# Transposing attention probabilities by DMA, and fetching sampled value rows with GpSimd gathers, in a fused BigBird attention and GELU feed-forward kernel

## The chip, the cores and the metric

The kernel runs on one core of a Trainium2 chip. The metric is the device time of one execution in microseconds (us). The core has a matrix engine (TensorE, PE in the profile), a vector engine (VectorE, DVE), an activation engine (ScalarE, ACT), GpSimd (POOL), and SyncE (SP), which here only issues DMAs. Every engine works through its own instructions in order; semaphores connect them. SP, ACT and POOL issue DMAs into queues that share 16 DMA engines.

## The reference

Inputs are q, k, v of shape (4 batches, 8 heads, 768 positions, 64), three sampled key blocks for each of the 24 query blocks of 32 positions, and two weight matrices. Everything is float32 outside; the kernel works in bf16 with float32 accumulation.

```python
scores = q @ k.T / sqrt(64)                    # for each batch and head
mask[i, j] = (|blk_i - blk_j| <= 1) | (blk_i in (0, 23)) | (blk_j in (0, 23))
mask[block qb, block kb] = True                # for kb in sampled_blocks[qb]
attn = softmax(where(mask, scores, -1e9))
x = (attn @ v)                                 # heads joined: 3072 x 512
out = gelu_exact(x @ w_in) @ w_out             # 512 -> 2048 -> 512
```

So the first and the last query block attend to all 768 keys (dense), and every other block attends to three neighbouring blocks, the two end blocks and three sampled blocks, 256 keys in all (sparse).

## The kernel before

The work is cut into eight units: four batches, two halves (`hf`) of 384 query positions. The order is written out by hand. For each unit an attention stage is followed by FFN1 (`ffn1_step`, 8 steps of 8 products with `w_in` and a Gelu on ACT); FFN2 of that unit (`ffn2_pieces`, 24 pieces of 2 products) is cut up as filler for the attention stage of the next unit. `ffn2_last` computes the last one.

A unit's attention has eight groups (`unit_groups`): two dense groups (the dense block, half of the heads each), then five groups of two sparse blocks and one of a single block. For each group:

- `stage_scores` (L309): PE multiplies q with keys into a PSUM tile `sc` of pool psA (two buffers); for sparse blocks the keys are a window of `kT` (96 columns) and `kg` (160 columns: three sampled and two end blocks). DVE takes the maximum (`nm`, L329 or L336).
- `stage_exp` (L340): ACT writes the exponentials `pp` in bf16 (L347, four of 256 columns; L350 for dense).
- `stage_transpose` (L353): PE transposes `pp` in squares of 128x128 against an identity into PSUM (`tp`, L359; 8 squares for two blocks, 6 for a dense group, 4 for one block).
- `stage_evict` (L362): ACT, or DVE at every fourth turn, copies `tp` to SBUF as `ps` (L367, L369).
- `stage_av` (L372): PE multiplies `ps` with values; a column of ones in the values gives the denominator. DVE normalizes into `xh` (L394 to L401).
- `stage_x` (L407): PE transposes `xh`, DVE copies it into `xT` (L421), the input of FFN1.

`attention` (L469) runs these as a software pipeline. In step `it`, PE gets the scores of group it+1, AV of group it-1, a filler piece, the transposes of group `it`, `stage_x` of group it-2 and another filler piece; ACT gets the eviction of group `it` and the exponentials of group it+1.

Values for the sparse groups lie in SBUF tiles `vg0s` and `vg1s`, one of each for each half. Each batch's values are copied to a DRAM scratch `vscr` (L257) from which `v_window` fetches the neighbouring blocks (L282) and `v_sampled` the sampled ones (L265): one DMA of 32 rows, 33 KB, for each sampled block, its address from a register that SP or POOL loaded from a list of block numbers (`numbers_list`, `registers`, L205). A sampled block that is already covered is replaced by the block of zeros behind the values. `v_ends` copies the end blocks (L272 to L277). The order of value rows in `vg0s` and `vg1s` is that of the keys: window, then sampled, then ends. Tiles of a half are refilled for the next batch while the other half is worked on: `v_fetch` gives lists of steps, some run in FFN1 (`steps`), the rest in the attention stage (`later`). For unit 1 this is `second_values` (L556), called in step 5 of FFN1 of unit 0. In FFN1 before a new batch (`fresh`), `prep_pair` (L217) transposes that batch's q and k on PE; `k_sampled` (L247) copies sampled keys into `kg` on DVE and POOL.

Of the kernel before, what the change touches and what calls it, by code (L numbers as in the profile page):

```python
# [20 lines left out]
def kernel(  # L21
# [27 lines left out]

    nc = tc.nc  # L50
    P = 128
# [5 lines left out]
    assert NR == 3  # L57
    D_MODEL, D_FF = moe_w_in.shape
# [16 lines left out]
    ptpool = ctx.enter_context(tc.tile_pool(name="ptpool", bufs=3))  # L75
# [3 lines left out]
    psT = ctx.enter_context(tc.tile_pool(name="psT", bufs=2, space=PSUM))  # L79
    psO = ctx.enter_context(tc.tile_pool(name="psO", bufs=1, space=PSUM))  # L80
# [74 lines left out]
    first_v = load_v(0)  # L155
    first_v[2]()
    load_k(0, HALVES[1])
    load_q(0, HALVES[1], slice(0, 64))
    for f in first_v[:2]:
        f()  # L160
    for i in range(2):
        nc.vector.memset(vns[i][:, :, :, D:VW], 1.0)
        nc.vector.memset(vgl[i][64:P, :, D:VW], 1.0)
# [28 lines left out]

    def numbers_list(src, js, rs, engine):
# [4 lines left out]
        return idx.rearrange("o j r -> o (j r)"), js, rs, engine, NB if src is vf else NB - 1  # L198
# [18 lines left out]
    def prep_pair(b, which, pr, on_act, p0=0, p1=P, bank=None):  # L217

        src = nats[which, b]
        pool, tag = bank or (psT, "T")  # L220
# [40 lines left out]
    def v_sampled(b, j, r):  # L261
        queue, val = (nc.gpsimd, v_pool[j, r]) if (j, r) in v_pool else (nc.sync, v_sp[j, r])
        hf, u = (j - 1) // US, (j - 1) % US
        dst = vg0s[hf][96:128, u, :] if r == 0 else vg1s[hf][BL * r - BL:BL * r, u, :]
        queue.dma_start(out=dst, in_=vscr[b][bass.ds(val * BL, BL), :])  # L265
# [13 lines left out]
    def v_window(b, hf, a, z, queue=None):  # L279

        r0 = (US * hf + a) * BL
        (queue or nc.sync).dma_start(  # L282
            out=vg0s[hf][0:96, a:z, :],
            in_=bass.AP(tensor=vscr[b].tensor, offset=vscr[b].offset + r0 * VR,
                        ap=[[VR, 96], [BL * VR, z - a], [1, VR]]))

    def v_fetch(b, hf):

        j0 = 1 + US * hf

        def sampled(js):
            for j in js:
                for r in range(NR):
                    v_sampled(b, j, r)

        moved = [lambda a=a: v_window(b, hf, a, min(a + 3, US)) for a in range(0, US, 3)]
        return moved, [lambda a=a: sampled(range(a, min(a + 2, j0 + US)))
                       for a in range(j0, j0 + US, 2)]
# [10 lines left out]
    def stage_scores(b, hf, grp):  # L309
# [8 lines left out]
        if grp[0] == "sparse":  # L318
            js = grp[1:]
            A4 = A.rearrange("p (g j c) -> p j g c", j=2, g=2)  # L320
            for i, j in enumerate(js):
                for c0, c1 in ((0, 96), (96, 256)):
                    for hh in range(4):
                        rhs = (kT[:, hh, (j - 1) * BL:(j + 2) * BL] if c0 == 0
                               else kg[:, (j - 1) % US, hh, :])
# [14 lines left out]
    def stage_exp(grp):  # L340
# [8 lines left out]
        else:  # L349
            nc.scalar.activation(pp[:, 0:S], A[:, 0:S], AF.Exp, bias=nm[:, 0:1])  # L350
        st[grp] = pp

    def stage_transpose(grp):  # L353
        pp = st[grp]
        T = psT.tile([P, 8, P], BF16, name="tp", tag="T")
        n = 4 * (len(grp) - 1) if grp[0] == "sparse" else NT
        for c in range(n):
            cols = slice(c * P, (c + 1) * P) if grp[0] == "sparse" else slice(c, S, NT)
            nc.tensor.transpose(T[:, c, :], pp[:, cols], identity)  # L359
        st[grp] = (T, n)  # L360

    def stage_evict(grp, on_act):  # L362
        T, n = st[grp]
        ps = ptpool.tile([P, 8, P], BF16, name="ps")
        turn[0] += 1
        if on_act or turn[0] % 4:
            nc.scalar.copy(ps[:, 0:n, :], T[:, 0:n, :])  # L367
        else:
            nc.vector.tensor_copy(ps[:, 0:n, :], T[:, 0:n, :])  # L369
        st[grp] = ps  # L370
# [36 lines left out]
    def stage_x(hf, grp):  # L407
# [13 lines left out]
        nc.vector.tensor_copy(  # L421
# [26 lines left out]
    def ffn2_last(b, hf):  # L448

        banks = [(psA, "A"), (psT, "T"), (psA, "A"), (psT, "T"), (psO, "O"), (psV, "av")]  # L450
# [18 lines left out]
    def attention(b, hf, filler, extra, steps=(), head=5, started=False):  # L469
# [3 lines left out]
        for it in range(-1, n + 2):  # L473
# [184 lines left out]
```

## Time and profile before

| | |
|---|---|
| time, median of 3 runs | 350.5 us (350.29 to 351.52) |
| profiled execution: time, span | 350.54 us, 348.6 us |
| busy share of the span | PE 86%, ACT 63%, DVE 55%, POOL 39% |
| mean granted TensorE clock | 0.946 (1.00 from about 60 us on) |
| DMA moved | 42.27 MB, 121 GB/s on average |
| attention stage, steady units | 24.7 to 26 us |
| FFN1 stage | 10.4 us, 15 us where the next batch is prepared |
| FFN2 of the last unit, to the end | 13.6 us |

The page is of one execution. Busy time of PE is not time at its peak, because products overlap in it. In a group line the columns are: line, engine, operation, output tile and input tiles, shapes, count, then busy time and mean duration of one, then idle time just before them and what ended it.

### The profile page before, as it was taken

The page shows a single profiled execution, that of the slowest core. Times are in us where ns is not written, and L with a number is a line of the kernel's source. Part 1 is how long each engine was busy: PE and PEld are TensorE (multiplying, and loading weights), DVE is VectorE, ACT ScalarE, POOL GpSimd, SP SyncE. Part 2 cuts the span into 40 slices and gives each one's busy share as a digit, 9 for nine tenths or more (in the row PEclk, how much of TensorE's full clock was granted, in tenths as well). Part 3 has the DMA queues.
Part 4 walks back from the last instruction along what each step waited for, and adds up shares of the span by engine and source line. Part 5 has one row for each costly group of instructions (what it writes and reads, how often), then busy time and mean ns, then how long its engine had stood idle before and what let it go on. Part 6 is the DMA issues. An engine that isn't in the chain of part 4 may idle for free.

```text
span 348.6 us, 13273 instructions
## 1 busy us (share of the span) xinstructions
PE 300.2 (86%) x5284; PEld 168.5 (48%) x5284; DVE 191.6 (55%) x569; ACT 221.3 (63%) x370; POOL 134.4 (39%) x269
## 2 busy tenths in 40 slices
PE   6456789986998889977998989997998989998996
PEld 5233445443553445444454445444554545454575
DVE  7395543673774765266473766276473764276100
ACT  2364725785467776786557885697567876778540
POOL 7767609901488271777400410966101310000000
PEclk9655659999999999999999999999999999999999
DMA  7949999898388935898870313996440310000002
GB/s 102 148 148 193 198 198 166 162 235 190 125 192 141 211 91 187 183 174 142 161 167 0 73 49 125 200 184 145 109 104 2 81 40 32 0 35 34 30 22 72
DMA packets 43807, 42.27 MB, mean 121 GB/s; under 512 B 7969, under 2 KB 38690, under 8 KB 43746
## 3 DMA queue, kind: packets, MB, share of 16 engines
q0 software_dynamic: 22528, 17.55, 32.3%
q1 hardware_dynamic: 20786, 23.48, 24.5%
q8 instruction: 41, 0.67, 0.8%
q10 hardware_dynamic: 432, 0.39, 0.3%
q14 instruction: 20, 0.16, 0.1%
HBM read 45.63 MB, written 9.67 MB: 159 GB/s over the span
## 4 chain that ended last, share of the span: by engine, by line
PE 51%; ACT 20%; DMA 10%; issue 9%; DVE 4%; SPq 4%; POOL 1%; DVEq 0%; ACTq 0%; POOLq 0%
PE hp L429 21%; PE op L438 13%; ACT pp L347 10%; DMA vg<-vscr 6%; ACT ps L367 4%; PE tp L359 4%; PE av L388 4%; SPq L265 3%; PE op L459 3%; PE pt L224 3%; DMA vx<-in_v_dram 3%; PE sc L314 2%; ACT os L443 2%; ACT g L431 2%; ACT L431 1%
## 5 line engine op out<-in xcount | busy, mean ns | idle before, releaser
L438 PE MATMUL op<-w_out_sb,g 128*128 128x512 bf16 x336 | 95.0, 381 | 2.2 <-ACT os L443 1.6
L429 PE MATMUL hp<-xT,w_in_sb 128*128 128x384 bf16 x512 | 91.8, 332 | 0.9 <-ACT g L431 0.6
L265 POOL DMA_DIRECT2D vg<-vscr x108 | 57.5, 537 | 55.6 <-issue 23.0
L431 ACT ACTIVATE g<-hp 128x768 bf16<-128x768 f32 x64 | 51.7, 811 | 37.5 <-PE hp L429 37.4
L347 ACT ACTIVATE pp<-sc,nm 128x256 bf16<-128x256 f32 x176 | 69.0, 488 | 0.1
L329 DVE TENSOR_REDUCE nm<-sc 128x4 f32<-128x1024 f32 (+1 forms) x48 | 54.5, 1136 | 26.1 <-ACT ps L367 9.8
L367 ACT COPY ps<-tp 128x1024 bf16<-128x1024 bf16 (+1 forms) x48 | 45.2, 941 | 36.9 <-PE tp L359 36.9
L429 PEld LDWEIGHTS <-w_in_sb 128*128 128x128 bf16 x512 | 48.8, 99 | 36.4 <-issue 5.7
L251 POOL COPY kg<-kT 128x128 bf16 x106 | 25.9, 293 | 64.5 <-PE sc L314 56.1
L359 PE MATMUL tp<-identity,pp 128*128 128x128 bf16 x448 | 44.7, 230 | 6.7 <-ACT pp L350 3.2
L359 PEld LDWEIGHTS <-pp 128*128 128x128 bf16 x448 | 31.4, 107 | 29.0 <-ACT pp L347 9.0
L388 PE MATMUL av<-vg,ps 128*32 128x65 bf16 x1408 | 22.9, 200 | 20.2 <-ACT ps L367 9.2
L336 DVE TENSOR_REDUCE nm<-sc 128x1 f32<-128x768 f32 x16 | 15.3, 955 | 44.6 <-PE sc L314 44.6
L388 PEld LDWEIGHTS <-ps 128*32 128x32 bf16 x1792 | 19.5, 98 | 35.8 <-ACT ps L367 20.9
L438 PEld LDWEIGHTS <-g 128*128 128x128 bf16 x336 | 24.8, 98 | 20.9 <-issue 11.3
L314 PE MATMUL sc<-kT,qT 64*32 64x96 bf16 (+2 forms) x832 | 27.6, 236 | 3.5 <-ACT qT L236 2.8
L314 PEld LDWEIGHTS <-qT 64*32 64x32 bf16 x1536 | 14.1, 93 | 31.6 <-issue 26.1
L443 ACT COPY os<-op 128x512 f32<-128x512 f32 x21 | 12.4, 593 | 25.8 <-PE op L438 25.8
L401 DVE TENSOR_TENSOR xh<-av,rec 128x256 bf16<-128x256 f32 (+1 forms) x64 | 22.9, 358 | 2.2
L234 DVE COPY kT<-pt 128x768 bf16<-128x768 bf16 x14 | 13.4, 956 | 16.5 <-PE pt L224 16.4
L394 DVE TENSOR_SCALAR den<-av 128x4 f32<-128x4 f32 (+1 forms) x64 | 9.9, 155 | 20.1 <-PE av L388 20.1
L314 PE MATMUL sc<-kg,qT 64*32 64x160 bf16 x704 | 18.2, 240 | 2.0 <-issue 1.8
(67 smaller groups left out, 277.5 us busy)
## 6 DMA issues: line engine op xcount, KB each, us to landing
vg<-vscr SPq DMA_DIRECT2D x20, 297.0 KB, 5.2
out_dram<-os SPq DMA_DIRECT2D x21, 256.0 KB, 2.1
vg<-vscr SPq DMA_DIRECT2D x156, 33.0 KB, 4.4
vg<-vscr POOLq DMA_DIRECT2D x108, 33.0 KB, 4.1
kn<-in_k_dram POOLq DMA_DIRECT2D x8, 384.0 KB, 6.4
vx<-in_v_dram POOLq DMA_DIRECT2D x8, 384.0 KB, 9.5
vscr<-vn SPq DMA_DIRECT2D x3, 792.0 KB, 3.3
qn<-in_q_dram POOLq DMA_DIRECT2D x6, 384.0 KB, 7.8
```

What stands on the lines that cost most here:

```text
L251: copy(kg[:, (j - 1) % US, :, BL * r:BL + BL * r], kTs[b % 2][:, :, bass.ds(vals[j, r] * BL, BL)])
L265: queue.dma_start(out=dst, in_=vscr[b][bass.ds(val * BL, BL), :])
L314: nc.tensor.matmul(out_, lhsT=qT[rows, h // 2, j * BL:(j + 1) * BL], rhs=rhs[rows], start=True, stop=True)
L329: nc.vector.tensor_reduce(out=nm[:, 0:2 * n].rearrange("p (j g) -> p j g", g=2), in_=A4[:, 0:n], op=ALU.max, axis=AX.X, negate=True)
L347: nc.scalar.activation(pp[:, 256 * n:256 * n + 256], A[:, c:c + 256], AF.Exp, bias=nm[:, n:n + 1])
L359: nc.tensor.transpose(T[:, c, :], pp[:, cols], identity)
L367: nc.scalar.copy(ps[:, 0:n, :], T[:, 0:n, :])
L388: nc.tensor.matmul(av[32 * hh:32 * hh + 32, s, :], lhsT=probs[:, 32 * hh:32 * hh + 32], rhs=vals[:, VW * h:VW * h + D + 1], start=(c == 0) ...
L401: nc.vector.tensor_tensor(xh[:, at:at + n, :], av[:, 0:n, 0:D], rec[:, 0:n, None].to_broadcast([P, n, D]), op=ALU.mult)
L429: nc.tensor.matmul(hp[:, i, 0:UT], lhsT=w_in_sb[:, ki, (m + i) * P:(m + i + 1) * P], rhs=xT[:, ki, :], start=(ki == 0), stop=(ki == KIN - 1))
L431: nc.scalar.activation(g[:, m:m + 2, :], hp[:, :, 0:UT], AF.Gelu)
L438: nc.tensor.matmul(op, lhsT=g[:, m, t * P:(t + 1) * P], rhs=w_out_sb[:, m, :], start=(m == 0), stop=(m == KOUT - 1))
```

## The change

- Probabilities: `stage_transpose` issues one transposing DMA on SP, from `pp` in SBUF to `ps` in SBUF (8, 6 or 4 squares at once). The PE transposes, the PSUM tile `tp` and `stage_evict` are gone. The dense exponentials are written in the order that the DMA needs.
- Pipeline: in step `it` the transposing DMA of group it+1 follows its exponentials, AV is of group it-2 and `stage_x` of group it-3; there is one step more. Two filler pieces come after AV in every step (four in the first). The copy to `xT` moves from DVE to ACT. ACT loads the Gelu table after the last exponentials of a unit.
- PSUM: psT has one buffer and psO two; `prep_pair` rotates over them.
- Sampled values: one indirect gather of POOL for each block, 96 rows, with row numbers computed on the chip (`value_rows`) in place of three DMAs with register addresses. Sampled rows now come first in the order (96 rows of `vg0s`), then the window (split over `vg0s` and `vg1s`, two DMAs), then the ends. Sparse scores are computed in three column slices (96, 96, 64) in place of two (96, 160).
- Order: values of unit 1 are fetched at the start of FFN1 of unit 0; loads of q and k move from the attention stage to FFN1; values of batch 0 are loaded with their end blocks last; some copies move between POOL and DVE.

```diff
-    ptpool = ctx.enter_context(tc.tile_pool(name="ptpool", bufs=3))
+    ptpool = ctx.enter_context(tc.tile_pool(name="ptpool", bufs=4))
...
-    psT = ctx.enter_context(tc.tile_pool(name="psT", bufs=2, space=PSUM))
-    psO = ctx.enter_context(tc.tile_pool(name="psO", bufs=1, space=PSUM))
+    psT = ctx.enter_context(tc.tile_pool(name="psT", bufs=1, space=PSUM))
+    psO = ctx.enter_context(tc.tile_pool(name="psO", bufs=2, space=PSUM))
...
-    first_v = load_v(0)
-    first_v[2]()
     load_k(0, HALVES[1])
     load_q(0, HALVES[1], slice(0, 64))
-    for f in first_v[:2]:
+    for f in load_v(0):
         f()
...
+    def value_rows():
+        vfb = const.tile([1, NB, NR], BF16, name="vfb")
+        nc.vector.tensor_copy(vfb, vf)
+        ones = const.tile([1, SW], BF16, name="ones")
+        nc.vector.memset(ones, 1.0)
+        seen = psV.tile([SW, NB, NR], F32, name="seen", tag="av")
+        nc.tensor.matmul(seen.rearrange("p j r -> p (j r)"), lhsT=ones,
+                         rhs=vfb.rearrange("p j r -> p (j r)"), start=True, stop=True)
+        for r in range(NR):
+            rows = slice(BL * r, BL * r + BL)
+            nc.vector.tensor_scalar(vrows[rows], seen[rows, :, r], float(BL), pcol[rows, 0:1],
+                                    op0=ALU.mult, op1=ALU.add)
...
-    def v_sampled(b, j, r):
-        queue, val = (nc.gpsimd, v_pool[j, r]) if (j, r) in v_pool else (nc.sync, v_sp[j, r])
+    def v_sampled(b, j):
         hf, u = (j - 1) // US, (j - 1) % US
-        dst = vg0s[hf][96:128, u, :] if r == 0 else vg1s[hf][BL * r - BL:BL * r, u, :]
-        queue.dma_start(out=dst, in_=vscr[b][bass.ds(val * BL, BL), :])
+        nc.gpsimd.indirect_dma_start(
+            out=vg0s[hf][0:SW, u, :], out_offset=None, in_=vscr[b][:, :],
+            in_offset=bass.IndirectOffsetOnAxis(ap=vrows[:, j:j + 1], axis=0))
...
-                for c0, c1 in ((0, 96), (96, 256)):
+                for c0, c1 in ((0, SW), (SW, 192), (192, 256)):
...
     def stage_transpose(grp):
         pp = st[grp]
-        T = psT.tile([P, 8, P], BF16, name="tp", tag="T")
+        ps = ptpool.tile([P, 8, P], BF16, name="ps")
         n = 4 * (len(grp) - 1) if grp[0] == "sparse" else NT
-        for c in range(n):
-            cols = slice(c * P, (c + 1) * P) if grp[0] == "sparse" else slice(c, S, NT)
-            nc.tensor.transpose(T[:, c, :], pp[:, cols], identity)
-        st[grp] = (T, n)
...
+        nc.sync.dma_start_transpose(out=ps[:, 0:n, :], in_=pp[:, 0:n * P])
         st[grp] = ps
...
-        nc.vector.tensor_copy(
+        nc.scalar.copy(
             xT[:, :, t0:t0 + n * BL].rearrange("p h (j q) -> p j h q", j=n),
...
-        for it in range(-1, n + 2):
+        for it in range(-1, n + 3):
             if it + 1 < n and not (started and it == -1):
                 stage_scores(b, hf, groups[it + 1])
-            if 0 <= it - 1 < n:
-                stage_av(b, hf, groups[it - 1])
-            for _ in range(head if it == -1 else int(it <= n)):
+            if 0 <= it - 3 < n:
+                stage_x(hf, groups[it - 3])
+            if 0 <= it - 2 < n:
+                stage_av(b, hf, groups[it - 2])
+            for _ in range(4 if it == -1 else 2):
                 next(filler, None)
-            if 0 <= it < n:
-                stage_transpose(groups[it])
-                stage_evict(groups[it], started and it < 3)
             if it + 1 < n:
                 stage_exp(groups[it + 1])
-            if 0 <= it - 2 < n:
-                stage_x(hf, groups[it - 2])
-            if it >= 0:
-                next(filler, None)
+                stage_transpose(groups[it + 1])
+            elif it + 1 == n:
+                nc.scalar.activation(warm, identity[:, 0:1], AF.Gelu)
...
     def second_values():
-        v_sp.update(block_numbers(vf, J1, (0, 1), SP))
-        for a in range(0, US, 4):
-            v_window(0, 1, a, min(a + 4, US))
-            for j in J1[a:a + 4]:
-                for r in range(NR):
-                    v_sampled(0, j, r)
+        moved, rows = v_fetch(0, 1)
+        for f in moved + rows:
+            f()
         for f in load_qk(1) + load_v(1):
             f()
...
             if u == 0:
                 k_dve |= block_numbers(ids, J1, (2,), DVE)
-                k_pool = block_numbers(ids, J1, (0, 1), POOL)
-                v_pool |= block_numbers(vf, J1, (2,), POOL)
+                k_pool |= block_numbers(ids, J1, (0, 1), POOL)
+                second_values()
...
-                if u == 0 and s == 5:
-                    k_dve |= block_numbers(ids, J0[5:], RS, DVE)
-                    second_values()
                 if s == 4 and nxt and not fresh:
                     v_ends(b, 1, nc.vector.tensor_copy)
+                if s == 6 and u > 0 and nxt and not fresh and b + 1 < B:
+                    v_ends(b + 1, 0, nc.vector.tensor_copy)
```

## Prediction

> **What bounds the kernel now.** I read the head of the page and its groups first, then one steady round in the timeline, then the DMA issues in a quiet and in a busy stretch, then the chain where it leaves its regular pattern. The groups that matter (instruction, tiles, shapes, count | busy us in all, mean ns | idle before, releaser):
>
> ```profile
> PE 300.2 (86%) x5284; PEld 168.5 (48%) x5284; DVE 191.6 (55%) x569; ACT 221.3 (63%) x370; POOL 134.4 (39%) x269
> ...
> L438 PE MATMUL op<-w_out_sb,g 128*128 128x512 bf16 x336 | 95.0, 381 | 2.2 <-ACT os L443 1.6
> ...
> L347 ACT ACTIVATE pp<-sc,nm 128x256 bf16<-128x256 f32 x176 | 69.0, 488 | 0.1
> ...
> L367 ACT COPY ps<-tp 128x1024 bf16<-128x1024 bf16 (+1 forms) x48 | 45.2, 941 | 36.9 <-PE tp L359 36.9
> ...
> L359 PE MATMUL tp<-identity,pp 128*128 128x128 bf16 x448 | 44.7, 230 | 6.7 <-ACT pp L350 3.2
> ```
>
> PE is busy 86% of the span. L347 and L367 show what ACT does in attention: exponentials, and three of four evictions of the transposed probabilities; their idle columns and that of L359 show ACT waiting for PE's transposes and PE for ACT's exponentials. A unit (one batch, half of the queries) is an attention stage of eleven loop steps, with FFN2 of the unit before as filler, and an FFN1 stage. From the first score product to the first FFN1 product the attention stages of units 0 to 7 last 29.7, 29.1, 26.9, 27.9, 25.9, 25.7, 25.9 and 24.7 us. Busy time of each engine in four steady rounds of unit 6, each from one group's first score product to the next group's:
>
> ```profile
> core 0: us, PE busy (x) PEld busy (x) DVE busy (x) ACT busy (x) POOL busy (x), PEclk, DMA share, GB/s
> 271.07:273.38 2.31, 2.23 (x69) 1.24 (x68) 1.63 (x4) 1.93 (x6) 1.00 (x4) 1.00 0.57 164
> 273.38:276.30 2.92, 2.52 (x78) 1.41 (x77) 2.25 (x6) 2.92 (x8) 1.00 (x4) 1.00 0.24 47
> 276.30:278.62 2.32, 2.30 (x79) 1.41 (x78) 2.16 (x6) 1.08 (x3) 1.00 (x4) 1.00 0.44 80
> 278.62:281.77 3.15, 2.73 (x79) 1.46 (x78) 2.64 (x7) 3.15 (x7) 1.00 (x4) 1.00 0.14 24
> ```
>
> Mean 10.70/4 = 2.68 us. In the two long rounds ACT is busy from end to end, as in
>
> ```profile
> 278.24 1.01 ACT L367 COPY ps<-tp 128x1024 bf16<-128x1024 bf16 x1 [1.24 <-PE tp L359]
> ...
> 279.15 1.57 ACT L347 ACTIVATE pp<-sc,nm 128x256 bf16<-128x256 f32 x4
> ```
>
> The eviction and the four exponentials are 2.6 of a round. The clock is 1.00 throughout.
>
> **Part by part, a steady round.** PE loses eight transposes. In the chain eight in a run take 0.46 us (121.02); 44.7 us over 56 such eights is 0.80, the rest being the wait for the last exponential. It gains 16 score products, since the slices are three now, not two: batches of eight start 0.06 to 0.07 us apart (271.07, 271.13, 271.20), so 0.15. What is left on PE: scores 0.5, AV 0.36, two filler pieces of 0.48 (ten FFN2 products in a run take 2.26), transposes of the output 0.1: 1.9 us. ACT loses an eviction of 1.01 in three rounds of four, and gains the copy to xT, which DVE does in 0.29; by the exponentials of the same width, four in 1.58, it is 0.4 on ACT. With the output's copy of 0.59 three times in ten rounds, ACT comes to 1.58 + 0.4 + 0.2 = 2.2. DVE, without its quarter of the evictions (0.69) and the xT copy, keeps the maximum 1.23, then 0.15 + 0.18 + 0.42 with gaps: 2.1. The engines are level, so I take 2.25 us a round, 0.43 less than now, over six rounds -2.6 us a unit.
>
> The price is the new path: exponentials, SP's issue, the transfer, AV. The trace has no transposing DMA. The nearest row is a store of as many bytes, 256 KB from SP, issue to landing, in unit 7's quiet stage (the DMA issues of 300 to 327 us; the last column is the landing):
>
> ```profile
> q1 hardware_dynamic: 432, 0.79, 7.7%
> ...
> out_dram<-os SPq DMA_DIRECT2D x3, 256.0 KB, 2.0
> ```
>
> and from 134 to 171 us, where loads for the next batch run:
>
> ```profile
> out_dram<-os SPq DMA_DIRECT2D x2, 256.0 KB, 6.3
> ```
>
> So 2.0 at the lower end. At the other end are pieces: a row of the source gives eight pieces of 256 bytes, 1024 in all. From the q1 line (packets, MB, share of 16 rings), 0.077 x 27 us x 16 / 432 = 77 ns a packet of 1.8 KB; over the whole span SP's and ACT's queue shows 0.245 x 348.6 x 16 / 20786 = 66 ns at about 1.1 KB. The straight line through both gives some 52 ns for 256 bytes, 64 pieces an engine: 3.3 us, and with issue and landing 5. I take 3.3 us from issue to landing, nearer the store, which is the same bytes from the same queue.
>
> Where that lands: AV of a group stands two rounds behind its exponentials in PE's order (loop index it+1 against it-2), so PE reaches it one round and the next scores later: 2.25 + 0.6 = 2.9 us after the exponentials end, if PE is on time. The loop from one end of exponentials through transfer, AV 0.36, fillers 0.95, scores 0.5, maximum 1.23, exponentials 1.58 and semaphores 0.3 spans four rounds: (3.3 + 4.9)/4 = 2.05, below 2.25. It decides only above 4.1 us. But at the end of a unit nothing is left to hide the last group's transfer: PE has two thin steps (AV 0.36, filler 0.95, output transposes 0.1: 1.4 each, 2.8) before that group's AV, which comes 3.3 and semaphores 0.3 after the exponentials. I charge 0.8. So -1.8 us a unit where DMA is quiet (units 2, 4, 6, 7): -7.2. In units 1, 3 and 5 the SP queue also carries value windows and POOL's gathers share the rings; I take half, -2.7. Behind a transpose that waits for its exponentials on SP stand the output stores and the windows; the stores are read by nobody, the windows only a unit later.
>
> The Trainium skill puts a transposing DMA at 261 GB/s where measured (DMA: Bandwidth & Descriptors, Latency and other measured facts), which would be 1.0 us of data for 256 KB, an estimate from that page; with the 2.0 of the store it would make 3.0 from issue to landing, 0.3 less at the end of seven units, so 336. No run here shows it yet.
>
> **Sampled values.** 264 transfers of 33 KB become 88 gathers of 96 rows, all from POOL. A gather costs POOL between 0.54 (one of today's issues) and 1.6 us (three of them); I take 0.9, as one 384 KB load costs 0.8 (537 ns is the mean of L265's 108 on POOL). From unit 2 on they run a unit ahead: no cost. Moved without cost too: the broadcast of the end blocks from POOL (4.58) to DVE (1.52), beside an FFN1 stage in which DVE is busy 2.0 of 9.0 us (134 to 143), and 54 key copies from DVE (0.20) to POOL (0.29), which has 40 us a unit; if POOL were late with them, PE would wait in the sparse scores. Unit 0: now the value copy in DRAM lands at 23.2 and POOL's first fetch goes at 23.9. After the change, POOL first waits for the two end blocks, now loaded behind the values (16.1), then does 0.62 + 4.58 + 4.38 us of copies, so gathers run from 26 to 37.6 with two weight loads between (33.6 or 45.3 at the ends), landing 4 us later; today's last AV is at 44.9. With a pipeline one round longer: +2, between 0 and +6. Unit 1 is where the chain leaves its pattern:
>
> ```profile
> 65.92 6.07 DMA vg<-vscr
> 72.01 5.78 DMA vg<-vscr
> 78.10 2.63 issue
> ```
>
> The fetches of unit 1 are issued from 62 us on, after register loads, and PE waits; its stage is 4.1 us longer than 25. The change issues them ahead of FFN1 of unit 0. But the loads for batch 1 then follow at once in POOL's queue, and the one for q must wait until the second half of q has been transposed at 60.9; POOL's 22 kg copies (5.25) stand behind it, and unit 1's sparse scores wait for those. I count -2. Unit 3 has one such wait of 1.9 at 159.6: -1. Loading the Gelu table ahead saves the 0.15 us PE stall in each FFN1: -1.
>
> **Sum.** The profiled execution was 350.54 (span 348.6 and 1.94 around it), the median 350.5: -7.2 - 2.7 + 2 - 2 - 1 - 1 = -11.9, so 338.5 us.
>
> **Rivals.**
> *Late transposes (slower).* The 6.3 us store shows what the SP queue does beside loads. If issue to landing is 5.5, the loop gives (5.5 + 4.9)/4 = 2.6 a round, +0.35 over six, and the end of the unit waits 2.2 more: 4.3 a unit over the forecast, seven units: 338.5 + 30 = 368. It decides from about 4.6 us on, where round and end together eat the 1.8. For it: median 4.4 us for the small fetches of today. Against: quiet stores at 2.0 in four units. 0.17.
> *Pieces bound the queue (slower).* At 3.3 us of ring time each, transposes go no faster than that: two dense ones of 2.5, five of 3.3, one of 1.7 make 23.2, with 3.4 ahead and 4 behind 30.6, 5.7 more than 24.9: about 350 + 8 x 5.7 = 396. 0.10.
> *Squares one by one.* If each 128x128 square were a transfer of its own after the last, at 1.3 us (the 1.9 us that a 33 KB fetch takes in quiet, less the landing that overlaps), 56 squares take 73 us a unit: about 350 + 8 x 50 = 750. 0.03. The Trainium skill's row for the DMA path, 1309 ns for one square against 390 on TensorE (VectorE: DVE Perf Modes, The three transpose paths), speaks for it; the trace's 2.0 us for eight times the bytes speaks against.
> *Gain given back on POOL.* Gathers of 1.6 us put unit 0 at +6, and unit 1 keeps its wait: 338.5 + 4 + 5 = 348 or a little more. 0.12, split evenly between a small gain, no change and a small loss.
>
> **How the numbers follow.** Forecast 0.58, its own range 322 to 347: the lower end if transposes land within 2.5 us and the rounds come down to the PE's 1.9. A measurement tells 0.5% (1.75 us) from no change. Faster: 0.57 of the forecast and 0.04 of the last rival, 0.61. Same: 0.01 and 0.04, 0.05. Slower: 0.17 + 0.10 + 0.03 + 0.04, 0.34. The range runs from just below the forecast's own to the queue-bound case, 320 to 398; the squares, half of the queue-bound case and a tail below are left out.
>
> **What would show it.** Right: no L359 or L367 left; steady rounds of 2.2 to 2.4 us; transposes landing in 3 to 4 us after issue; PE waiting for ps only at a unit's end; unit 1's stage under 28. Wrong: AV waiting for the transposes in every round, SP's issue rows lasting over 2 us, or the first FFN1 product of unit 0 after 50 us.

## The result, and the profile after

The changed kernel takes 488.9 us (median of four runs, 481.8 to 493.1) where the kernel before takes 351.0 beside it: a ratio of 1.383, with a 95% interval of 1.359 to 1.407. The ratio counts only runs within 1.5% of the fastest of their kernel (481.8 and 488.7 us here; 356.3 us is left out before), and so do all ratios below. The forecast was 338.5 us, and the range ended at 398. The profiled execution took 493.05 us with a span of 491.0, the longest of the four; two later profiles of the same kernel (486.4 and 484.1 us) show the same rows.

The page of the changed kernel, engines first, then groups (line, engine, operation, tiles, count | busy us in all, mean ns | idle before, releaser):

```profile
PE 295.1 (60%) x5485; PEld 160.4 (33%) x5541; DVE 177.0 (36%) x447; ACT 241.2 (49%) x386; POOL 158.6 (32%) x300
...
L285 POOL DMA_INDIRECT vg<-vscr,vrows x88 | 83.0, 943 | 158.8 <-issue 73.4
...
L446 PE MATMUL op<-w_out_sb,g 128*128 128x512 bf16 x280 | 88.9, 442 | 12.8 <-issue 12.8
...
L368 ACT ACTIVATE pp<-sc,nm 128x768 bf16<-128x768 f32 x16 | 58.2, 3709 | 35.2 <-DVE nm L354 33.6
...
L396 PE MATMUL av<-vg,ps 128*32 128x65 bf16 x1408 | 22.2, 208 | 52.9 <-DMA ps<-pp 52.1
L354 DVE TENSOR_REDUCE nm<-sc 128x1 f32<-128x768 f32 x16 | 15.3, 955 | 96.3 <-remote 62.7
```

TensorE still has some 300 us of work, now in 491. Its mean granted clock is 0.80 where it was 0.95, and an FFN2 product (L446) lasts 442 ns in place of 381, so a part of each loss below can be the lower clock. L359 and L367 are gone. Three things took their place. The dense exponentials (L368) last 3.71 us each; before the change they lasted 0.90 (count, shortest, median and longest in ns, first and last start, shapes):

```profile
L350 ACT ACTIVATE pp<-sc,nm x16: 882/904/907, 19.7 to 304.3; 128x768 bf16<-128x768 f32 x16
```

AV (L396) stands idle 52 us for the transposing DMA. And the dense maxima (L354) wait 63 us for "remote", which no instruction or transfer in the trace explains. The waits for the DMA are few and long. These are the two longest pieces of that kind in the chain that ended last (start, duration):

```profile
48.17 29.13 DMA ps<-pp x2
...
302.63 11.98 DMA ps<-pp
```

The attention stages of units 0 to 7, from the first score product to the first FFN1 product, last 65.0, 35.6, 44.8, 37.2, 46.6, 38.0, 37.4 and 32.2 us; before the change none was over 31. FFN1 of unit 1, with gathers beside it, lasts 27.4 us in place of 14.5. (Read in the same way, unit 0 took 30.7 us before, not the 29.7 of the prediction.)

### The profile page after: what moved, and what is told of

Read it like the earlier page. It is cut to its first block, busy times and chain, and to the rows that moved or that the text cites. A ratio compares the mean times of both kernels' runs of the same rounds, so it can differ in the third digit from the quotient of the medians.

```text
span 491.0 us, 13019 instructions
## 1 busy us (share of the span) xinstructions
PE 295.1 (60%) x5485; PEld 160.4 (33%) x5541; DVE 177.0 (36%) x447; ACT 241.2 (49%) x386; POOL 158.6 (32%) x300
## 4 chain that ended last, share of the span: by engine, by line
PE 33%; DMA 22%; another core or an unknown queue 17%; DVE 10%; ACT 10%; issue 6%; DVEq 1%; POOL 0%; POOLq 0%; SPq 0%; ACTq 0%
DMA ps<-pp 21%; PE hp L437 15%; PE op L446 7%; ACT pp L368 5%; PE av L396 3%; ACT pp L365 3%; DVE nm L354 3%; PE sc L331 2%; PE op L467 2%; DVE kg L273 2%; PE pt L246 2%; DVE nm L347 2%; PE tx L426 1%; ACT os L451 1%
## 5 line engine op out<-in xcount | busy, mean ns | idle before, releaser
L285 POOL DMA_INDIRECT vg<-vscr,vrows x88 | 83.0, 943 | 158.8 <-issue 73.4
L446 PE MATMUL op<-w_out_sb,g 128*128 128x512 bf16 x280 | 88.9, 442 | 12.8 <-issue 12.8
L368 ACT ACTIVATE pp<-sc,nm 128x768 bf16<-128x768 f32 x16 | 58.2, 3709 | 35.2 <-DVE nm L354 33.6
L331 PE MATMUL sc<-kg,qT 64*32 64x96 bf16 (+1 forms) x1408 | 31.6, 228 | 69.5 <-ACT pp L368 43.6
L273 POOL COPY kg<-kT 128x128 bf16 x160 | 39.7, 299 | 76.8 <-DVE kT L256 43.4
L331 PEld LDWEIGHTS <-qT 64*32 64x32 bf16 x2240 | 25.6, 100 | 112.1 <-issue 62.3
L396 PE MATMUL av<-vg,ps 128*32 128x65 bf16 x1408 | 22.2, 208 | 52.9 <-DMA ps<-pp 52.1
L354 DVE TENSOR_REDUCE nm<-sc 128x1 f32<-128x768 f32 x16 | 15.3, 955 | 96.3 <-remote 62.7
L396 PEld LDWEIGHTS <-ps 128*32 128x32 bf16 x1792 | 21.2, 107 | 72.6 <-DMA ps<-pp 65.6
L446 PEld LDWEIGHTS <-g 128*128 128x128 bf16 x336 | 29.5, 107 | 39.0 <-issue 19.3
L429 ACT COPY xT<-tx 128x256 bf16<-128x256 bf16 (+1 forms) x56 | 19.7, 352 | 45.9 <-PE tx L426 45.7
L331 PE MATMUL sc<-kT,qT 64*32 64x96 bf16 (+2 forms) x832 | 33.6, 253 | 6.8 <-ACT qT L258 3.0
L426 PE MATMUL tx<-identity,xh 128*128 128x128 bf16 x96 | 16.2, 240 | 10.1 <-DVE xh L409 6.9
L258 ACT ACTIVATE qT<-pt 128x768 bf16<-128x768 bf16 (+1 forms) x16 | 11.6, 730 | 18.8 <-PE pt L246 14.4
```

Source lines behind the costliest of these rows:

```text
L273: copy(kg[:, (j - 1) % US, :, BL * r:BL + BL * r], kTs[b % 2][:, :, bass.ds(vals[j, r] * BL, BL)])
L285: nc.gpsimd.indirect_dma_start(out=vg0s[hf][0:SW, u, :], out_offset=None, in_=vscr[b][:, :], in_offset=bass.IndirectOffsetOnAxis(ap=vrows[ ...
L331: nc.tensor.matmul(out_, lhsT=qT[rows, h // 2, j * BL:(j + 1) * BL], rhs=rhs[rows], start=True, stop=True)
L354: nc.vector.tensor_reduce(out=nm[:, 0:1], in_=A[:, 0:S], op=ALU.max, axis=AX.X, negate=True)
L368: nc.scalar.activation(pp[:, 0:S].rearrange("q (t p) -> q p t", t=NT), A[:, 0:S].rearrange("q (p t) -> q p t", t=NT), AF.Exp, bias=nm[:, 0:1])
L396: nc.tensor.matmul(av[32 * hh:32 * hh + 32, s, :], lhsT=probs[:, 32 * hh:32 * hh + 32], rhs=vals[:, VW * h:VW * h + D + 1], start=(c == 0) ...
```

## The experiments

Eighteen runs were made on five chips, A to E; those on one chip were made one after another. The kernel before took 350.7 to 352.6 us on each of them, so ratios can be compared between chips. One thing cannot, as will be seen. Stage lengths are read as above. "Pauses" are idle times of TensorE of over 0.3 us, beside a gather, ahead of an instruction that waits for nothing; how near to a gather still counts moves a sum by some us.

### One part undone at a time (chip A)

**Dense exponentials in rows.**

```
-  pp[:, 0:S].rearrange("q (t p) -> q p t", t=NT), A[:, 0:S].rearrange("q (p t) -> q p t", t=NT)
+  pp[:, 0:S].rearrange("q (t p) -> q t p", t=NT), A[:, 0:S].rearrange("q (p t) -> q t p", t=NT)
```

> The changed kernel with one edit: the dense exponentials write 128 consecutive elements at a time and read every sixth element of PSUM, in place of the reverse. Theory: the 16 exponentials of 3.71 us (0.90 before) lie on the path at the head of each unit; they fall to 0.9 to 1.2 us and the time falls by 16 x 2.6 = 42 us, to 440 to 455. Rival, that the head of a unit waits for the late reduces and transposes anyway: the exponentials fall as far, the time by under 15 us. Rival, that ACT is as slow over a strided read as over a strided write: they stay over 3 us and the time at 482 to 493.

430.5 us, ratio 1.220 (1.209 to 1.231), some 10 us under the theory's range; the chip turned out to have a part in that. The group of this kernel:

```profile
L368 ACT ACTIVATE pp<-sc,nm 128x768 bf16<-128x768 f32 x16 | 14.4, 898 | 14.7 <-DVE nm L354 14.3
```

The same elements, written side by side and read with a stride from PSUM, cost 0.90 us. The strided bf16 write was the whole of the 2.8 us by which one exponential had grown.

**Plain transfers for the gathers.**

```
-  nc.gpsimd.indirect_dma_start(out=vg0s[hf][0:SW, u, :], ..., in_offset=IndirectOffsetOnAxis(ap=vrows[:, j:j + 1], axis=0))
+  nc.gpsimd.dma_start(out=vg0s[hf][0:SW, u, :], in_=vscr[b][(j - 1) * BL:(j + 2) * BL, :])
```

> The changed kernel with each gather replaced by a plain transfer of 96 neighbouring rows on the same queue; it leaves the choice of rows out, with the same bytes into the same places. Theory: the indirect form holds up DVE and PE (62.7 us of waits of the dense reduces that no engine's work explains, 15.9 and 17.3 in two other rows); they go and the time falls by 50 to 90 us, to 400 to 440. Rival, that the load of 100 KB per gather on the rings is what delays everything: the waits stay and the time is 475 to 495. Rival in between, that only POOL's 0.94 us per gather is gained: 2 to 8 us in units 0 and 1, 480 to 487.

443.6 us, ratio 1.263 (1.255 to 1.270), just above the theory's range, and no remote wait is left. I took this for the theory. Most of the 45 us was the chip: the changed kernel never ran on this one, and the repeats below show what that means.

**Squares on TensorE again, straight after their exponentials.** `stage_transpose` as before the change with the eviction behind it, dense exponentials in plain order, psT with two buffers and psO with one.

> The changed kernel with the squares transposed on TensorE and evicted by ACT and DVE again, with the PSUM banks as before the change and the dense exponentials in plain order; the gathers and the schedule stay. Theory of three losses: the waits for the transposing DMA (60.9 us) and the slow exponentials (45 us) go, the stalls beside the gathers stay (60 to 90 us), PE and ACT have more to do: 385 to 430. Rival, that the transposing DMA is the cause of all three: 340 to 365 with no unexplained waits of the reduces. Rival, that the gathers are: over 440.

432.7 us, ratio 1.233 (1.226 to 1.240). It says little: TensorE reached each group's transposes while ACT was still at its exponentials, and every stage, also that of unit 7 with nothing beside it (34.6 us), was long. The kernel further down with the transposes one round later is the proper undo.

**Both of the first two.**

> The dense exponentials written in rows and the gathers replaced by plain transfers of 96 neighbouring rows (the choice of rows left out), the transposing DMA kept. Theory: the two losses add up, 488 - 42 - 50 to 90 = 356 to 396, and what is left over 350 is the transposes delayed behind other transfers. Rival, that they overlap (the slow exponentials hide behind the stalls): within 10 us of the better of the two kernels that have one edit each.

424.3 us, ratio 1.207 (1.200 to 1.214). Beside each other on one chip, the exponentials are worth 19.3 us here (443.6 to 424.3) and the indirect form 4.5 (ratio 1.220 to 1.207). What is left, 73 us over the kernel before, is neither. Two windows of this kernel's DMA issues, unit 0 and then unit 7 (queues: packets, MB, share of 16 engines; issues: count, median us to landing):

```profile
q0 software_dynamic: 5264, 5.70, 55.8%
q1 hardware_dynamic: 9968, 4.88, 51.7%
...
ps<-pp SPq DMA_TRANSPOSE x8, 14.6
```

```profile
q1 hardware_dynamic: 7734, 2.41, 55.1%
...
ps<-pp SPq DMA_TRANSPOSE x8, 4.0
```

Beside the weights on POOL's queue a transpose takes 14.6 us from issue to landing, alone 4.0. Stages: 63.6 us for unit 0, 25.1 for unit 7.

### Again, and the traffic (chip B)

**The changed kernel again.**

> The changed kernel itself once more, for a second trace. The two edits so far were worth 58 and 45 us alone and 65 together, so what the profile calls remote waits of the dense reduces (62.7 us) went with either. Theory: these waits are real in every execution and need both the slow exponentials and the gathers: 480 to 493, with 40 us or more of such waits again. Rival: they are a feature of that one profiled execution, whose trace lacks 56 of 5541 matmuls: the waits of the reduces are for TensorE and under 50 us, and the time is 475 to 490.

485.2 us, ratio 1.383 (1.376 to 1.390), with 46.0 us of remote waits of the dense maxima and all 5541 matmuls in the trace: the waits are no artefact of one profile.

**Windows on POOL's queue**, dense exponentials in rows (`nc.sync` to `nc.gpsimd` in `v_window`).

> The kernel with the dense exponentials in rows (430.5 us) and one more edit: the windows of values are issued on POOL's queue, so that SP's queue holds transposes, the copies to the scratch and the outputs. Theory A, the transposes wait in SP's ring behind windows of 0.33 to 0.4 MB: landings of 5 to 11 us in units 3 and 5 fall under 5 us and the time falls to 405 to 420. Theory B, all queues share the 16 engines, whichever ring the bytes are in: within 6 us of 430.

449.6 us, ratio 1.281 (1.272 to 1.290): slower than its partner on chip A, where it should have been equal or faster. The trace has 38 us of pauses against 0.9 in the partner. Inconclusive, as the two chips differ; it was repeated with plain transfers.

**No values for batches 1 to 3** (`if b: return` in `v_scratch`, `v_sampled` and `v_window`), dense exponentials in rows.

> The kernel with the dense exponentials in rows (430.5 us) without the scratch copies, windows and gathers of values for batches 1 to 3 (left out; these units read the rows of batch 0); the loads of k, q and v stay. Theory: what delays the transposes in units 2 to 7 is the traffic of values beside them; these six units, 192.6 us in that kernel, fall to 25 to 27 each, 156 us, and the time to 385 to 400, still over the kernel before because of units 0 and 1. Rival: the loads of k, q and v and SP's 1.2 us per issue delay them: 412 to 430.

403.8 us, ratio 1.150 (1.141 to 1.158), 4 us above the theory's range; its partner ran on chip A. Units 3, 5, 6 and 7 come to 25.2, 25.7, 26.6 and 23.5 us; units 2 and 4 stay at 31.8 and 36.6. So it is not the values alone.

**Squares on TensorE one round later, gathers kept.** `stage_transpose(groups[it])` stands between the fillers and the exponentials of group it+1; `xT` is copied on DVE.

> The changed kernel with the squares on TensorE again, one round after their exponentials as before the change, the xT copies back on DVE, the dense exponentials in plain order and the PSUM banks of before; what stays of the change is the gathers, the placing of the loads, the new order of the start and AV one round later. The kernel with the squares straight after the exponentials took 432.7 us with 34.6 to 42.5 us per attention stage. Theory: in that one TensorE waited for each exponential, and all that the gathers cost beside loads is in unit 0: 355 to 375. Rival, that the gathers hold up each unit: over 385. Rival, that they gain as they were meant to: under 351.

428.4 us, ratio 1.220 (1.214 to 1.227). It seemed to show that the gathers alone cost 78 us. TensorE's timeline in unit 5, with gathers running (start, duration, [idle before <-releaser]):

```profile
286.86 0.23 PE L331 MATMUL sc<-kg,qT 64*32 64x64 bf16 x6
287.61 0.21 PE L331 MATMUL sc<-kg,qT 64*32 64x64 bf16 x2 [0.52 <-issue]
289.02 0.25 PE L331 MATMUL sc<-kg,qT 64*32 64x96 bf16 x4 [1.20 <-issue]
291.14 0.28 PE L331 MATMUL sc<-kg,qT 64*32 64x96 bf16 x3 [1.88 <-issue]
292.55 0.23 PE L331 MATMUL sc<-kg,qT 64*32 64x96 bf16 x1 [1.12 <-issue]
293.27 0.24 PE L331 MATMUL sc<-kT,qT 64*32 64x96 bf16 x1 [0.49 <-issue]
```

Score products that come eight at a time elsewhere come by one to six, at multiples of some 0.7 us, without a wait, until the last gather's bytes have landed.

### The same kernels on a third chip, and one part alone (chip C)

**Dense exponentials in rows, again.**

> The kernel with the dense exponentials in rows once more, on the same chip as the next three. It took 430.5 us on another chip than the kernel with the squares on TensorE one round later (428.4 us), and its TensorE had no pauses without a wait beside the gathers (0.9 us in all) where that one's had 33.7 us. Theory, pauses are a matter of when the gathers fall: 425 to 440 again, under 3 us of pauses. Rival, they are a matter of the chip: 445 to 475 with 20 us of pauses or more here, if the kernel with the squares on TensorE has them here again.

433.7 us, ratio 1.217 (1.205 to 1.228), 2.5 us of pauses: as on chip A.

**Squares on TensorE one round later and plain transfers**: both edits shown above.

> The squares on TensorE one round after their exponentials, and plain transfers of 96 neighbouring rows in place of the gathers (the choice of rows left out): of the change there remain the placing of the loads, the order of the start and AV one round later. With the gathers this kernel took 428.4 us, 34.6 to 36.7 us per attention stage of a unit with gathers beside it and 25.4 in the one without. Theory, the indirect form holds up all engines: 25 to 29 us in units 1 to 7 and 352 to 370 in all. Rival, that it is the load or the schedule: over 400. Rival in between, that half of it is the load: 375 to 400.

366.3 us, ratio 1.041 (1.033 to 1.048), in the theory's range. Units 3, 5 and 7 last 25.5 us, but units 1, 2 and 4 last 32.7, 29.5 and 29.4, above its 25 to 29: the loads that now run there cost time without any transposing DMA.

**The kernel before with the transposing DMA alone**: squares by DMA right after the exponentials, AV in step `it` of group it-2, `ptpool` with four buffers.

> The kernel before with the transposing DMA alone: squares by DMA right after the exponentials, dense exponentials in rows, AV one round later, four buffers of transposed squares; values are fetched as before, by register-addressed transfers. Theory, transposes wait behind other transfers: 25 us stages where the rings are quiet, 3 to 8 us more per unit beside the fetches of values, and 15 to 30 us more in unit 0 beside the weights: 385 to 420. Rival, the forecast's reasoning without the gathers: 335 to 345. Rival in between, that only unit 0 loses: 360 to 380.

447.1 us, ratio 1.259 (1.246 to 1.271), worse than with the rest of the change on this chip (the kernel above with the exponentials in rows, 1.217) and above the range. In unit 4 the transposes land within 2.8 to 4.8 us and the stage still lasts 36.1. SP's timeline there:

```profile
266.54 1.66 SPq L359 DMA_TRANSPOSE ps<-pp  x1
268.39 2.37 SPq L265 DMA_DIRECT2D vg<-vscr  x4
270.88 1.26 SPq L359 DMA_TRANSPOSE ps<-pp  x1
```

The old row fetches stand in SP's order between two transposes, and SP issues almost without a break from 259 to 285 us. Moving them to POOL is thus rather a condition of the transposes than a second gain.

**Squares on TensorE one round later, with gathers, again.**

> The kernel with the squares on TensorE one round later and the gathers, once more, on the same chip as the three beside it. Theory, pauses go with the placing of the gathers: 425 to 432 with 30 us or more of pauses without a wait on TensorE. Rival, they go with the chip: where the first of these four has none, neither has this one, and it takes 370 to 400.

369.7 us, ratio 1.050 (1.043 to 1.058), where the same kernel took 428.4 on chip B. The rival came true (0.3 us under its range). One row of both, chip B first, then this chip:

```profile
L381 ACT COPY ps<-tp 128x1024 bf16<-128x1024 bf16 (+1 forms) x48 | 45.2, 941 | 75.4 <-remote 44.4
```

```profile
L381 ACT COPY ps<-tp 128x1024 bf16<-128x1024 bf16 (+1 forms) x48 | 45.2, 941 | 40.8 <-PE tp L377 40.6
```

The remote waits and the pauses belong to the indirect gathers on some chips: 33.7 us of pauses on B, 6.3 on C. (Each chip stands for one occasion, so whatever else differed between two occasions goes under the same name.) On C the gathers cost 3.4 us more than plain transfers. And on this one chip, with gathers in both, the step from squares on TensorE to the transposing DMA (ratio 1.050 to 1.217) is 59 us.

### Which part is the chip's, which the queue's (chip D)

**The changed kernel a third time, and the rows beside it.**

> The changed kernel itself, on one chip with the three beside it. The kernel with the squares on TensorE and the gathers took 428.4 us on one chip, with 33.7 us of pauses of TensorE without a wait, and 369.7 us on another, with 6.3 us; so some of the changed kernel's 485 to 489 us can be the chip that it ran on. Theory: without the pauses it takes 455 to 475, the slow dense exponentials alone being 30 to 42 us over the kernel with them in rows. Rival: it takes 480 to 492 on this chip too, and the pauses come with the slow exponentials.

478.0 us, ratio 1.344 (1.331 to 1.357), between the two ranges.

> The kernel with the dense exponentials in rows, as the partner of the changed kernel on the same chip: 426 to 441 where TensorE has no pauses beside the gathers, as on two chips so far; 445 to 475 with over 15 us of pauses if this chip is one that has them.

464.9 us, ratio 1.321 (1.311 to 1.332), with 34.6 us of pauses; the changed kernel has 22.8. D is a chip with pauses. By the ratios they cost this kernel some 36 us against A and C (1.220 and 1.217). On D the slow exponentials are worth only 8 us (1.344 to 1.321); that the heads of the units wait there anyway would explain it, and is not shown. The changed kernel ran on no chip without pauses; from chip A, 424.3 + 19.3 + 4.5 = 448 us is my estimate for one, so 24 to 37 us of its three measurements (1.344 to 1.383 times 351) are pauses.

**Windows on POOL's queue, plain transfers, exponentials in rows.**

> Dense exponentials in rows and plain transfers in place of the gathers (the choice of rows left out; 424.3 us, no pauses), and the windows of values issued on POOL's queue. Theory A, the transposes wait in SP's ring behind windows, as the order of the ring has it: units 0, 2 and 4 (63.6, 42.9 and 40.6 us) fall to 40, 32 and 30, and the time to 380 to 398. Theory B, the bytes share the 16 engines whichever ring they are in: 412 to 428.

414.2 us, ratio 1.177 (1.169 to 1.185), against 424.3 with the windows on SP: theory B's range. Unit 0 falls from 63.6 to 50.8 us, units 2 and 4 stay at 43.6 and 39.5, and unit 1 rises from 31.7 to 42.2, since the loads of batch 1 now stand further back in POOL's queue and run beside its transposes. Net of both, and across two chips, the order in SP's ring is worth some 10 us.

**Deeper buffers, on top of that** (the edit in short).

```
-  ppool bufs=3, ptpool bufs=4;  stage_av(groups[it - 2]), stage_x(groups[it - 3])
+  ppool bufs=5, ptpool bufs=6;  stage_av(groups[it - 3]), stage_x(groups[it - 4])
```

> The kernel beside it with the windows on POOL's queue, and room for later landings: five buffers of probabilities in place of three, six of transposed squares in place of four, AV one more round behind. Theory, what is left are single landings of 4 to 8 us, which two more rounds hide: 10 to 25 us less than the kernel beside it. Rival, the rings are full over whole stretches, and lag hides nothing of that: within 5 us of it. Rival, that the longer drain at the end of each unit costs 8 times 1 to 2 us: up to 12 us more.

399.8 us, ratio 1.136 (1.125 to 1.146). The exponentials of the kernel beside it, then of this one:

```profile
L363 ACT ACTIVATE pp<-sc,nm 128x256 bf16<-128x256 f32 x176 | 69.8, 482 | 46.6 <-DMA ps<-pp 28.7 <-DVE den L400 7.8 <-issue 6.6
```

```profile
L363 ACT ACTIVATE pp<-sc,nm 128x256 bf16<-128x256 f32 x176 | 69.2, 482 | 14.9 <-DVE nm L345 14.7
```

The exponentials' waits for a transpose to land (28.7 us, because three buffers of `pp` are only free when their transposes have landed; all of them in units 0 to 5) are gone. Stages of units 3, 5 and 7: 25.3, 23.2 and 23.5 us. Buffers and the later AV came together, so their shares are open.

### What the transposes want (chip E)

**No transfers beside them after unit 1**: the kernel above with `nats` of batch 0 used for all batches and `if b: return` as before.

> The kernel with plain transfers, windows on POOL's queue and deeper buffers (399.8 us) without the loads of k, q and v and the scratch copies, windows and row transfers of batches 1 to 3 (left out; these batches read batch 0's inputs). Theory, what delays the transposes after unit 1 is any large transfer beside them: units 2 to 7, 170.3 us there (34.7, 25.3, 38.7, 23.2, 24.9, 23.5), take 23 to 24.5 each, and the time falls to 365 to 378, units 0 and 1 being as before. Rival, it is the transposes' own issue on SP and their 1024 packets each: units 2 and 4 stay over 30 us, 385 to 400.

355.3 us, ratio 1.014 (1.007 to 1.021), 10 us below the expected range, because unit 1 becomes quiet too: 25.2 us. Units 2 to 7 last 23.7, 23.7, 24.9, 23.8, 24.5 and 23.1 us, all with the same transposes in the same number of packets as in the kernel above, where units 2 and 4 took 34.7 and 38.7. Unit 4 above, then here (window, length, busy us of each engine with counts, TensorE clock, DMA share, GB/s):

```profile
225.00:263.80 38.80, 24.18 (x571) 10.98 (x566) 14.81 (x40) 18.15 (x40) 14.42 (x37) 0.80 1.01 153
```

```profile
193.80:218.70 24.90, 20.38 (x567) 9.66 (x566) 14.57 (x39) 17.82 (x40) 5.64 (x22) 1.00 0.65 106
```

What made the transposes late was the other transfers. Not all of the 44 us is theirs, though: the kernel before and the one with squares on TensorE were not run without these loads. The latter's units 1, 2 and 4, 15 us longer together than three of its 25.5, suggest some 15 us that the loads cost in any case (an estimate).

**The kernel before, with transposes by DMA in the last unit only.**

```
+  if nxt == units[-1]:   # squares by DMA, rows, AV of group it-3, ppool 5, ptpool 6
+      attention_dma(b, hf, filler)
```

> The kernel before with the transposing DMA in the last unit alone, where no load or fetch is beside it: squares by DMA, dense exponentials in rows, AV two rounds later, five and six buffers. Theory, a quiet unit gains what the deeper kernel showed, 24.7 to 23.5: 1.0 to 1.6 us less, 349 where the kernel before takes 350.5, ratio 0.995 to 0.998. Rival, the longer drain before the last FFN and the Gelu table take it back: ratio 0.999 to 1.003.

347.9 us against 351.9: ratio 0.989 (0.984 to 0.993), a gain of 1.1%, clear of noise and larger than both expectations. It is the fastest kernel of the study. The stage of unit 7 in the kernel before, then here:

```profile
299.40:324.10 24.70, 22.56 (x534) 11.62 (x534) 16.35 (x41) 18.56 (x35) 0.00 (x0) 1.00 0.07 24
```

```profile
299.30:321.80 22.50, 19.25 (x477) 8.49 (x476) 15.49 (x39) 15.51 (x32) 0.00 (x0) 1.00 0.75 115
```

PE has 3.3 us less to do, ACT 3.0, and the stage is 2.2 us shorter, at a DMA share that goes from 0.07 to 0.75. The two traces differ by 2.6 us of span; for the rest of the 4.0 they show no place.

## Why the prediction was wrong

**Steady round, 2.68 to 2.25 us: right in size, for a quiet unit with more buffers.** The prediction took 1.8 us off a quiet unit. With five buffers of `pp` and AV a round later unit 7 became 2.2 us shorter than before in the last kernel, 1.2 and 1.6 in the two with the change's own loop (23.5 and 23.1 against 24.7). With the change's three buffers and its AV it gained nothing (25.1 us and 24.7 in the two kernels with plain transfers). The step that failed is the loop, which was to decide only above 4.1 us: at a median landing of 4.0, AV of unit 7 waits 3.5 us for its squares, 2.1 of them before the unit's end (kernel with both edits). The loop also left out a shorter way, in which a buffer of probabilities is free only when its transpose has landed; that one cost time beside loads, in units 0 to 5.

**The transfer, 3.3 us between 2.0 and 5: right alone, not beside loads.** A transpose of 256 KB with nothing near takes 2.7 us to land; its median in a quiet unit is 4.0 (two in a row overlap) and its 1024 packets take 18 ns each, not the 52 ns of the straight line. The case in which pieces bound the queue was not what happened. By the Trainium skill's 261 GB/s (DMA: Bandwidth & Descriptors, Latency and other measured facts) the data take 1.0 us, an estimate from that page; the trace has 1.08 us from first to last packet, which agrees.

**Quiet units 2, 4, 6 and 7: the step that failed most.** I took the list of quiet units from the trace of before. The change puts the loads of v into the attention stages of units 2 and 4 (before, they ran in units 2 and 3), and the loads of k and q, written in the next FFN1, start on POOL while the last transposes of those units fly: in unit 4 of the kernel with both edits they are issued at 263.3 to 265.5, and the chain there holds one wait of 12.1 us for a transpose, from 264.5 on. The loads of that stretch, and the two longest waits for a transpose in the chain of unit 4:

```profile
kn<-in_k_dram POOLq DMA_DIRECT2D x2, 384.0 KB, 7.3
qn<-in_q_dram POOLq DMA_DIRECT2D x2, 384.0 KB, 11.9
```

```profile
247.66 7.52 DMA ps<-pp
264.47 12.06 DMA ps<-pp
```

Units 2 and 4, which I credited with -1.8 us each, become 18 and 21 us longer (16 and 15 in the kernel with both edits, 2.6 and 3.5 with squares on TensorE and plain transfers). Units 1, 3 and 5, credited with half, become 2.6, 0.4 and 4.3 us longer with both edits. The rival of late transposes had the right mechanism and the right point (landing above 4.6 us), but its price of 4.3 us a unit stood on one landing of 5.5, not on 10 to 12 at the end of a unit.

**Unit 0, +2 between 0 and +6: the largest single term, mis-sized.** The first FFN1 product comes at 83.0 us in place of 46.7. With squares on TensorE it comes at 52.9 (plain transfers) or 55.0 (gathers, chip C), so the new order and the gathers alone are 6 to 8 us. I costed the gathers there and not the transposes: 4 MB of weights share the rings with them. POOL's 5264 packets in the window shown take 0.558 x 65 x 16 / 5264 = 110 ns each; if each of the 64 packets that a transpose has per engine waits for one of those, that is 7 us (an estimate), and SP's own windows come on top. With the windows taken off SP's ring unit 0 falls from 63.6 to 50.8 us. The Trainium skill says that an engine takes its queues in turn, a packet at a time (DMA: Bandwidth & Descriptors, Queues, rings and completion order). Its packets are groups of descriptors and need not be those that the profile counts. The landings of 14.6 us beside 55.8% of other traffic fit such turns, and no run here shows the turns themselves.

**Dense exponentials: costed at nothing, and nowhere named.** 2.8 us each, 8 to 19 us in all. The change said that their write order was new, and I did not look up its price. The Trainium skill has a rule for it (SBUF — State Buffer, Door 1: The DMA port swizzle): accesses that cross to another 16-byte line pay. 3.71 us against 0.90 agrees with that.

**Gathers at 0.9 us on POOL: right (0.94), and beside the point.** On A and C they are worth 3 to 5 us, within the forecast. On B, D and in the first result TensorE, ACT and DVE stand still beside them, 24 to 37 us by the estimate above, up to 59 in the same kernel on two chips. Nothing in the trace of before could show it, but its nearest row, a direct issue, was the wrong kin for an indirect form that had never run in this kernel.

**Units 1 and 3, and the Gelu table (-2, -1 and -1).** The kernel with squares on TensorE and plain transfers shows these apart from the transposes. Unit 1 lasts 32.7 us in place of 29.1 there, so its wait did not go (35.6 in the changed kernel, where under 28 was to be the sign of being right); unit 3 lasts 25.5 in place of 27.9, better than forecast; FFN1 in four units lasts 10.6 in place of 10.9, as forecast.

**What would show it.** No L359 or L367: yes. Rounds of 2.2 to 2.4: only around 2.6 in unit 7 of the kernel with rows. Landing in 3 to 4 us: in quiet stages only. AV waiting at unit ends only: no, 24 waits, 61 us. SP issues over 2 us and the first FFN1 product of unit 0 after 50 us, both named as signs of being wrong, came.

In sum, on chips without pauses: what else changed, the order of start and loads above all, 14 us (the kernel with squares on TensorE and plain transfers, 366.3 against 352.6), the transposing DMA 58 (366.3 to 424.3, across two chips; 59 on chip C alone), the exponentials 19, the gathers 5; then 24 to 37 us of pauses. The parts were measured on chips A and C, whose common kernel differs by 3 us. Of the 58, some 10 are the order in SP's ring and 14 the missing buffers and lag. The rest, and more, goes when no load runs beside the transposes, but that run also takes away what the loads cost by themselves. So the change lost instead of gaining 12 us because of its transposes beside loads above all, and of two costs that the prediction did not have, the strided write and the pauses.

## What to carry to other kernels

A transfer that replaces engine work has to be costed in the stage that it lands in, with the loads that the changed kernel, not the old one, has there: the one here needed a quiet stage, buffers on both of its sides, and a queue with no other issues in between. Ask the price of every access pattern that a change rewrites. Repeat one kernel on a second chip before a difference between kernels is put down to an edit.

## What was not expected of the hardware

- Beside indirect gathers from POOL, TensorE, ACT and DVE stand still on some chips (B and D) and hardly on others (A and C): one program, 428.4 and 369.7 us. During the pauses the clock is granted (1.00 until TensorE has idled), the DMA share is 0.2 to 0.4, and instructions are hardly fetched (one packet in 10 us of pauses in unit 5 on chip B). Why is open. Beside the same 96 rows by a plain transfer, chip D included, no engine has a remote wait, and such idle times of TensorE come to 3 us at most in a kernel.
- A bf16 exponential over 768 columns takes 0.90 us when it writes side by side and reads every sixth PSUM element, 3.71 us the other way round.
- 256-byte packets of a transposing DMA take 18 ns each with nothing beside them; beside the weights of unit 0 their mean is 45 ns (kernel with both edits), and a landing goes from 2.7 to over 14 us.
